# Weight decode through a PSUM bank, a scaling moved to ScalarE, and a new plan of the order, in a fused attention and two-MLP kernel

## The chip, the cores and the metric

One core of one Trainium2 chip runs the whole program. The metric is the device time of one execution in microseconds (us); smaller is better. Engines in the rows: PE is TensorE (PEld its weight loads), DVE VectorE, ACT ScalarE, POOL GpSimd, SP SyncE, which here issues every DMA. An engine name with a q is its instruction queue.

## The reference

Attention with a forget bias, for 4 batches, 8 heads, 576 positions and a head size of 64; then two MLPs over the 2304 tokens of width 512:

```python
cum = np.cumsum(np.maximum(s, 0.0), axis=-1)
scores = scale * q @ k.T + np.minimum(-(cum_q - cum_k), 0.0)     # masked causally
x = softmax(scores) @ v                                          # heads side by side: 2304 x 512
h = x @ w_in                                                     # 512 x 1024
solu = h * softmax(h)
ln = (solu - mean) / sqrt(var + 1e-6) * g_ln
x = ln @ w_out                                                   # 1024 x 512
h = max(x @ w1, x @ w2, x @ w3)                                  # 512 x 768 each
out = h @ w_out2                                                 # 768 x 512
```

The MLP weights arrive as 64-bit floats. The kernel reads each as two 32-bit integers and builds the 32-bit float from them; then it splits it into a high and a low fp16 half, and each product is three fp16 products (high by high, high by low, low by high).

## The kernel before, in words

**Tiles.** The tokens are cut into 18 tiles of 128. A pair of batches has 9: for each of four key blocks j, one tile of either batch, then a tail tile with the last 64 tokens of both. So tiles 0 to 3 use only the first two key blocks. Two tiles make a group; there are 9 groups.

**Steps of a tile.** `prep` (L606) loads q, k and v, splits them into halves (`split_ops`, L370: scaling to the high half L384, L386; low half L413 on DVE or L420 and L423 on POOL) and transposes q and k by DMA (L618, L628). `scores` (L658) makes the products (L684, L690) and the maximum pass (L721, L754). `half` (L764) does the exponential (L773), the split and the transpose by DMA (L792). `values` (L806) multiplies by v (L836, L849), normalizes (L883, L877), splits and transposes (L891). `m1` (L900) is x @ w_in (L915), softmax and LayerNorm (L929 to L977), a split and a transpose by DMA (L984). **Steps of a group:** `m2` (L987: product with w_out L1006, halves L433 and L1023), `m3` (L1027: products with w1, w2, w3 L1045, first result copied L433, running maximum L1064, split), `m4` (L1070: product with w_out2 L1079, output).

**Weights.** `load_w` (L510) handles 40 pieces of 128 x 512 floats (512 KB each): 8 of w_in, 8 of w_out, 18 of w1 to w3 ("w3" in names; piece f, i is columns f of matrix i, in the order f, then i) and 6 of w_out2 ("w2o"). A piece lands in one of four staging buffers, which are halves of the K and V storage (tiles kt and vs in the rows) that belong to key blocks 2 and 3; token tile 4 is the first to store keys there. Three passes on DVE put the bits together: dec1 (L527) into a wide work buffer, a tile of the pool "f" of three; dec2 (L530) in that buffer; dec3 (L533) back into the staging buffer. `split_ops` then scales the staging buffer to the high half (ACT, DVE or POOL) and makes the low half (DVE L413 or POOL L420, L423). w_out is scaled by g_ln, a value per partition, the others by a constant.

**Prologue.** `prologue` (L450) loads s, scales it and cuts it at zero (L474 on DVE), scans it (L476), splits it into three bf16 parts (L483, L486) and writes them to DRAM (L488), from where `load_c` (L491) reads them as operands of the score products. POOL meanwhile fills constants (L459 to L470).

**PSUM.** Eight banks: two for scores (sc), one for values (av), two for h, and three (pool "acc", not first in first out) for m2, m3 and m4. An m3 bank holds one matrix for two columns f: 24 products, 12 for each of two weight pieces.

**The order.** `build` (L331) lists operations with their engines, durations in ns, what they read and write, and a due position `pos` in units of token tiles. `Schedule.run` (L141) plays them on a model: of what could start within `look` ns of the earliest start on an engine it takes the lowest `pos`; where several engines can do an operation, `spare` adds to each engine's end time before it chooses (three numbers up to the position `spare_until`, three after it). Buffers of a pool are given out as they become free. Operations that use the SBUF port which DVE and POOL share in this model are kept apart in time, except the kinds listed in `ALONE` (L96). The resulting order is written out per engine, so each engine runs a fixed list; a waiting instruction holds what stands behind it on its engine, DMA issues on SP too. `P` (L30) holds the positions: wi, wo, w3, w4 the first piece of w_in, w_out, w1 to w3 and w_out2 and wid, wod, w3d, w4d the step from piece to piece; la, lp, lu, lv attention, o1 to o4 and ds the MLP steps, mp the LayerNorm.

Of the kernel before, what the change touches and what calls it, by code (L numbers as in the profile page):

```python
# [29 lines left out]
P = dict(  # L30
    la=4.705,
    lp=-0.544,
    lu=2.19,
    lv=-2.704,
    o1=0.295,
    o2=-2.196,
    o3=1.33,
    o4=0.194,
    ds=2.217,
    wi=-8.083,  # L40
    wid=-0.055,
    wo=0.504,
    wod=1.507,
    w3=-3.448,
    w3d=1.657,
    w4=-4.056,
    w4d=3.311,
    mp=1.816,
    look=[0.0, 0.0, 0.0, 315.4, 20.3],
    spare=[1717.6, 14.8, 1096.8, 262.7, -659.2, -218.5, 5.6],  # L50
    n_st=4,
    avn=1,
    gs=[2, 2, 2, 2, 2, 2, 2, 2, 2],
# [3 lines left out]
    nr=3,  # L57
    lc=-0.912,
    S=[],
# [32 lines left out]
class Schedule:  # L92
    LAT_SAME, LAT_CROSS, LAT_DMA, LAT_ISSUE = 130, 180, 930, 650


    ALONE = frozenset("ttr m1max m3x xn x2l x2h m3c ob rec scan m1v gs".split())  # L96

# [8 lines left out]

    def op(self, alts, reads, writes, pos, dma=0, kind=""):

        o = Op()
        o.unit = self.unit + "." if dma else self.unit  # L110
        o.cls = f"{kind}@{self.tile}"
        only = self.eng.get(o.cls)
        o.alts = [(e, int(ns + 0.5), f) for e, ns, f in alts if not only or e[0] in only]
        o.base, o.dma, o.kind = pos, int(dma + 0.5), kind
        o.pos = pos + self.off.get(o.unit, 0.0)
        o.index = len(self.ops)
        o.deps, o.after, o.bufs = set(), set(), {}
        for k in reads:
            o.deps.update(self.last.get(k, ()))
            self.readers.setdefault(k, []).append(o)  # L120
        for k in writes:
            if k in self.readers or k in self.last:
                o.deps.update(self.readers.get(k, ()))
                o.deps.update(self.last.get(k, ()))
            self.last[k] = [o]
            self.readers[k] = []
        for k in list(reads) + list(writes):
            b = k[0] if isinstance(k, tuple) else k
            if isinstance(b, Buf):
                self.hold(o, b)  # L130
        o.deps.discard(o)
        self.ops.append(o)
        return o
# [7 lines left out]
    def run(self):  # L141
# [6 lines left out]
        dma = 0  # L148
        port = [0]
        busy, warm = {}, [False]  # L150

        def ports(o, e):

            return e == "POOL" or e == "DVE" and o.kind not in self.ALONE

        def clock(t, ns):
# [93 lines left out]
        for _ in self.ops:  # L250
# [10 lines left out]
            t, o, i, e = best  # L261
            ns, o.fn = o.alts[i][1:]
            o.start, o.eng = t, e
            if o.dma:
# [66 lines left out]
def build(nc, T, X, dims):  # L331
# [22 lines left out]
    op = S_.op  # L354
    pools = {}
    for name, n, fifo in (
# [5 lines left out]
        ("mn", 4, True), ("den", 2, True), ("st8", 2, True),  # L362
        ("sc", 2, True), ("av", P["avn"], True), ("h", 1, True), ("acc", 4 - P["avn"], False),
    ):
# [85 lines left out]
    def prologue():  # L450
# [16 lines left out]
        def tri():  # L467
# [5 lines left out]
        op([("POOL", 500, tri)], ["maskt"], ["maskt"], p0, kind="mask")  # L473
        op([("DVE", 369, lambda: nc.vector.tensor_scalar(  # L474
            out=spt(), in0=spt(), scalar1=S_MUL, scalar2=0.0, op0=ALU.mult, op1=ALU.max))], [sp], [sp], p0, kind="relu0")
        op([("DVE", 669, lambda: nc.vector.tensor_tensor_scan(  # L476
# [33 lines left out]
    def load_w(src, hi, lo, scale, pos, wkey, extra=()):  # L510
# [6 lines left out]
        for i in range(nsrc):  # L517
# [7 lines left out]


        op([("DVE", dve1(512), lambda: nc.vector.tensor_scalar(  # L527
            out=t(), in0=high(), scalar1=3, scalar2=0x3FFFFFF8,
            op0=ALU.logical_shift_left, op1=ALU.bitwise_and))], sk, [tb], pos, kind="dec1")
        op([("DVE", dve2(512), lambda: nc.vector.scalar_tensor_tensor(  # L530
            out=t(), in0=low(), scalar=29, in1=t(), op0=ALU.logical_shift_right, op1=ALU.bitwise_or))],
           sk + [tb], [tb], pos, kind="dec2")
        op([("DVE", dve2(512), lambda: nc.vector.scalar_tensor_tensor(  # L533
            out=low(), in0=high(), scalar=-(1 << 30), in1=t(), op0=ALU.bitwise_and, op1=ALU.bitwise_or))],
           sk + [tb], sk, pos, kind="dec3")
        split_ops(lambda g: hi, lambda g: lo, lambda g: low().bitcast(F32), scale, 512,
                  sk + list(extra), [(wkey, 0), (wkey, 1)], pos, k="w", scaled=scaled("w"))

# [119 lines left out]
    def scores(t, h0):  # L658
# [71 lines left out]
        for n, (lo, hi) in enumerate(((0, KH), (KH, S))):  # L730
            sc = [buf("sc") for _ in range(2)]

            def f_sc(n=n, lo=lo, hi=hi, sc=sc):
# [15 lines left out]
               [qt] + ["ktail"] * n + [("kt", i, 2 * n + x) for i in range(2) for x in range(2)] + keyed,  # L749
               sc, pos, kind="sc")  # L750
            for y in range(2):
# [148 lines left out]
    def m1(t):  # L900
# [74 lines left out]
        def ts(eng):  # L975
# [8 lines left out]
        op([("SP", 625, lambda: nc.sync.dma_start_transpose(out=lnt(), in_=lnb()))],  # L984
           [(lnb, 0), (lnb, 1)], [(lb, o)], pos, dma=1792, kind="lnT")

# [141 lines left out]
def fox_attention_solu_max3_kernel(  # L1128
# [59 lines left out]
    for name, n, shape, dt in (  # L1188
# [8 lines left out]
        T[name] = [mk(f"{name}{i}", shape, dt) for i in range(n)]  # L1197
    for name, n, w in (("sc", 2, 512), ("av", P["avn"], 512), ("h", 1, DFF), ("acc", 4 - P["avn"], 512)):
        T[name] = [mk(f"{name}{i}", [128, w], F32, psum) for i in range(n)]
# [39 lines left out]
```

## Time and profile before

| | |
|---|---|
| time before, median of 3 runs | 693.94 us (691.15 to 696.44) |
| the profiled execution's own time | 692.71 us |
| its span in the profile | 690.9 us |
| busy: PE, DVE, ACT, POOL | 598.7, 426.8, 349.4, 107.9 us |
| mean granted TensorE clock | 0.975 of full speed |

The page gives busy time over the whole span, and 40 slices of 17.3 us each, in which a digit is the busy share in tenths. A stage view gives the same for chosen stretches: for each engine the busy us and the number of instructions, then the granted clock, the mean busy share of the 16 DMA engines and what they moved. A group row gives how often an instruction ran, its busy time in all and the mean of one in ns, then the idle time of its engine just before it and what ended that. In a timeline row the first number is the start, the second the duration; instructions on one engine overlap a little, so starts can be closer than durations.

### The profile page before, as it was taken

The numbers are of one execution on the slowest core, as the hardware profiler recorded it, in microseconds if no ns is written. First come the engines' busy times: TensorE is split into PE (matmuls) and PEld (weight loads), VectorE is DVE, ScalarE is ACT, GpSimd is POOL, SyncE is SP. The second block draws the span as 40 slices with busy tenths as digits, with TensorE's granted clock in tenths as the row PEclk, the third lists the DMA queues.
The fourth block names the chain that finished last, engine by engine and source line by source line (L and its number), as shares of the span: only waits on it lengthen the run. The fifth ranks groups of instructions, "written<-read, shape, count | busy, mean of one in ns | idle before, by whom it ended". The sixth has DMA issues, their size and how long they took to land.

```text
span 690.9 us, 15166 instructions
## 1 busy us (share of the span) xinstructions
PE 598.7 (87%) x6028; PEld 425.2 (62%) x6028; DVE 426.8 (62%) x970; ACT 349.4 (51%) x784; POOL 107.9 (16%) x132
## 2 busy tenths in 40 slices
PE   0126658969889999999999999999999999999997
PEld 0012326747456657866676667676867686786784
DVE  6899899998767764747287538733774253143121
ACT  1457665356667763737475638633853244144111
POOL 4003300010103312333133103001121010000000
PEclk9999767989999999999999999999999999999999
DMA  6999998658999994788899947753665040210201
GB/s 174 238 259 242 185 235 203 193 139 191 180 163 171 168 197 91 116 134 145 161 185 177 173 94 129 132 93 62 128 97 96 32 81 16 56 32 8 48 15 31
DMA packets 283016, 91.07 MB, mean 132 GB/s; under 512 B 259136, under 2 KB 277760, under 8 KB 282944
## 3 DMA queue, kind: packets, MB, share of 16 engines
q1 hardware_dynamic: 282944, 90.10, 66.2%
q8 instruction: 47, 0.77, 0.5%
q14 instruction: 25, 0.20, 0.1%
HBM read 35.95 MB, written 4.83 MB: 59 GB/s over the span
## 4 chain that ended last, share of the span: by engine, by line
PE 52%; DMA 23%; DVE 13%; ACT 4%; issue 3%; SPq 3%; POOL 1%; DVEq 0%; ACTq 0%
PE acc L1045 20%; PE acc L1006 9%; DMA et<-es 9%; PE h L915 8%; DMA lnt<-ln 4%; PE acc L1079 4%; PE sc L690 4%; PE av L849 3%; PE sc L684 2%; DVE f L530 2%; DVE es L413 1%; DMA kt<-in_moe_w_dram 1%; PE av L836 1%; DMA ett<-est 1%; DMA raw<-in_q_dram 1%
## 5 line engine op out<-in xcount | busy, mean ns | idle before, releaser
L1045 PE MATMUL acc<-x2A,w_h 128*128 128x256 f16 x1296 | 218.8, 274 | 6.9 <-DVE w_h L413 5.2
L1045 PEld LDWEIGHTS <-w_h 128*128 128x128 f16 x1944 | 187.1, 98 | 39.1 <-DVE w_h L413 6.1
L1045 PE MATMUL acc<-x2B,w_h 128*128 128x256 f16 x648 | 177.5, 274 | 0.0
L915 PE MATMUL h<-w_in_h,xt 128*128 128x512 f16 x432 | 106.4, 393 | 12.0 <-DMA xt<-xs 11.9
L1006 PE MATMUL acc<-lnt,w_out_h 128*128 128x256 f16 x864 | 98.9, 276 | 12.5 <-DMA lnt<-ln 11.7
L773 ACT ACTIVATE r<-r,mn 128x128 f32<-128x128 f32 (+4 forms) x144 | 82.7, 575 | 41.1 <-DVE mn L721 28.7
L1006 PEld LDWEIGHTS <-w_out_h 128*128 128x128 f16 x864 | 84.8, 99 | 26.8 <-issue 12.8
L413 DVE SCALAR_TENSOR_TENSOR es<-r,es 128x512 f16<-128x512 f32 (+1 forms) x92 | 65.9, 723 | 24.7 <-ACT es L384 21.3
L915 PEld LDWEIGHTS <-xt 128*128 128x128 f16 x432 | 40.6, 100 | 60.3 <-DMA xt<-xs 12.9
L384 ACT ACTIVATE es<-r 128x512 f16<-128x512 f32 (+1 forms) x94 | 54.1, 585 | 32.0 <-DMA et<-es 31.3
L721 DVE CUSTOM_DVE_ANT_0 r<-sc,mask 128x128 f32<-128x128 f32 (+3 forms) x128 | 58.1, 485 | 17.4 <-PE sc L690 16.2
L849 PE MATMUL av<-vs,et 128*128 128x64 f16 x960 | 39.5, 197 | 29.9 <-DMA et<-es 28.7
L1079 PE MATMUL acc<-w2o_h,h2A 128*128 128x512 f16 x216 | 64.3, 379 | 0.0
L1064 DVE TENSOR_TENSOR f<-f,acc 128x512 f32<-128x512 f32 x54 | 36.9, 684 | 43.5 <-PE acc L1045 41.7
L849 PEld LDWEIGHTS <-et 128*128 128x128 f16 x960 | 35.7, 100 | 38.4 <-DMA et<-es 32.2
L1023 DVE SCALAR_TENSOR_TENSOR x2B<-acc,x2A 128x512 f16<-128x512 f32 x18 | 12.4, 689 | 64.2 <-ACT x2A L433 64.1
L684 PE MATMUL sc<-ckr,cqr 6*128 6x128 bf16 (+5 forms) x192 | 27.0, 312 | 25.1 <-DMA cqr<-cum_d 24.3
L690 PE MATMUL sc<-kt,qt 64*128 64x256 f16 (+2 forms) x768 | 48.3, 268 | 0.0
L433 ACT ACTIVATE x2A<-acc 128x512 f16<-128x512 f32 x18 | 10.7, 596 | 62.2 <-PE acc L1006 62.2
L1079 PE MATMUL acc<-w2o_h,h2B 128*128 128x512 f16 x108 | 40.9, 379 | 0.0
L384 ACT ACTIVATE h2A<-f 128x512 f16<-128x512 f32 x25 | 15.6, 626 | 47.3 <-DVE f L1064 47.3
L690 PEld LDWEIGHTS <-qt 64*128 64x128 f16 (+1 forms) x864 | 27.2, 100 | 15.9 <-issue 9.1
(111 smaller groups left out, 718.9 us busy)
## 6 DMA issues: line engine op xcount, KB each, us to landing
kt<-in_moe_w_dram SPq DMA_DIRECT2D x18, 256.0 KB
vs<-in_moe_w_dram SPq DMA_DIRECT2D x18, 256.0 KB
raw<-in_k_dram SPq DMA_DIRECT2D x16, 256.0 KB
raw<-in_q_dram SPq DMA_DIRECT2D x16, 256.0 KB
raw<-in_v_dram SPq DMA_DIRECT2D x16, 256.0 KB
out_dram<-f SPq DMA_DIRECT2D x16, 256.0 KB
vs<-in_moe_w_out_dram SPq DMA_DIRECT2D x7, 512.0 KB
kt<-in_moe_w_out_dram SPq DMA_DIRECT2D x7, 512.0 KB
```

Source lines behind the costliest of these rows:

```text
L384: eng.activation(out=out(g), in_=src(g), func=AF.Copy, scale=sc(g))
L413: nc.vector.scalar_tensor_tensor(out=lo(g), in0=src(g), scalar=sc1(g), in1=hi(g), op0=ALU.mult, op1=ALU.subtract)
L684: yield lambda: nc.tensor.matmul(out=out(), lhsT=T["cqr"][cr, hp, cs], rhs=T["ckr"][cr, hp, ck], start=True, stop=False, skip_group_check= ...
L690: yield lambda n=n, qa=qa, o=o, kx=kx: nc.tensor.matmul(out=out()[:, o], lhsT=qv()[r, qa * HP + hp, ts], rhs=kx, start=False, stop=(n == 2 ...
L721: nc.vector.tensor_tensor_reduce(out=gw(R)[:, g], in0=gw(sc[y])[:, g], in1=T["mask"][:, SM - W:SM], scale=1.0 / S_MUL, scalar=3e38, op0=AL ...
L773: nc.scalar.activation(out=gw()[:, g], in_=gw()[:, g], func=AF.Exp, bias=mnf()[:, g:g + 1], scale=-1.0, accum_out=den(hs[g]),)
L849: nc.tensor.matmul(out=out, lhsT=ea_[:, ea, kb], rhs=T["v_s"][c, kb // 2][:, kb % 2, ha + a, va], start=(kb == 0 and m == 0), stop=(kb == ...
L915: nc.tensor.matmul(out=hb()[:, n * 512:(n + 1) * 512], lhsT=xt()[:, xa, kk], rhs=T["w_in_h"][:, wa, kk, n * 512:(n + 1) * 512], start=(kk ...
L1006: nc.tensor.matmul(out=ps()[:, d % 2 * GN:(d % 2 + 1) * GN], lhsT=T["w_out_h"][:, wa, kk, d * 128:(d + 1) * 128], rhs=lnt()[:, la, kk], st ...
L1045: nc.tensor.matmul(out=ps()[:, f % 2 * GN:(f % 2 + 1) * GN], lhsT=T["w123_h"][:, w, wa, f, kk], rhs=x2(xa)[:, kk], start=(kk == 0 and i == ...
L1064: op([("DVE", dve2(2 * GN), lambda ps=ps: nc.vector.tensor_tensor(out=m(), in0=m(), in1=ps(), op=ALU.max))], pk + [m], [m], pos, kind="m3x")
L1079: nc.tensor.matmul(out=ps(), lhsT=h2(ha)[:, f, o * 128:(o + 1) * 128], rhs=T["w2o_h"][:, wa, f], start=(f == 0 and i == 0), stop=(f == KF2 ...
```

## The change

1. In `load_w` dec2 writes an "acc" PSUM bank instead of the work buffer, dec3 works in that bank, and both halves are made from it: the high half on ACT only, the low half on DVE only. The work buffer is read last by dec2, the staging buffer by dec3.
2. The first scaling of s runs on ACT as a Relu with a scale.
3. The planner's model: switching TensorE between score products and other products costs 95, 150 or 300 ns; DMA latency is 1250 instead of 930 ns; the LayerNorm transpose takes 2200 instead of 1792 ns; dec3 and the low half ("wl") no longer count as users of the shared port.
4. All positions in `P` are new, and so is the order of everything.

The pool of "av" was of size P["avn"] = 1 and is now written as 1, "acc" as 3.

```diff
 P = dict(
-    la=4.705, lp=-0.544, lu=2.19, lv=-2.704,
-    o1=0.295, o2=-2.196, o3=1.33, o4=0.194, ds=2.217,
-    wi=-8.083, wid=-0.055, wo=0.504, wod=1.507,
-    w3=-3.448, w3d=1.657, w4=-4.056, w4d=3.311, mp=1.816,
-    look=[0.0, 0.0, 0.0, 315.4, 20.3],
-    spare=[1717.6, 14.8, 1096.8, 262.7, -659.2, -218.5, 5.6],
+    la=10.467, lp=-3.933, lu=3.473, lv=-4.007,
+    o1=-5.042, o2=-6.852, o3=2.269, o4=0.122, ds=5.562,
+    wi=-14.577, wid=-2.374, wo=-5.08, wod=-0.141,
+    w3=0.541, w3d=0.309, w4=-4.008, w4d=5.211, mp=-0.033,
+    look=[0.0, 0.0, 0.0, 213.2, 19.2],
+    spare=[2262.6, -562.2, 1965.8, 458.7, -1447.5, 987.2, 10.4],
...
-    LAT_SAME, LAT_CROSS, LAT_DMA, LAT_ISSUE = 130, 180, 930, 650
+    LAT_SAME, LAT_CROSS, LAT_DMA, LAT_ISSUE = 130, 180, 1250, 650
-    ALONE = frozenset("ttr m1max m3x xn x2l x2h m3c ob rec scan m1v gs".split())
+    ALONE = frozenset("ttr m1max m3x xn x2l x2h m3c ob rec scan m1v gs dec3 wl".split())
...
+        def turn(o, e):
+            if e != "PE" or (o.kind == "sc") == (rows[0][:2] == "sc"):
+                return 0
+            return 95 if o.kind == "sc" else 300 if rows[0] == "sct" else 150
...
             ns, o.fn = o.alts[i][1:]
+            t = max(t, free[e] + turn(o, e))
...
-        op([("DVE", 369, lambda: nc.vector.tensor_scalar(
-            out=spt(), in0=spt(), scalar1=S_MUL, scalar2=0.0, op0=ALU.mult, op1=ALU.max))], [sp], [sp], p0, kind="relu0")
+        op([("ACT", 640, lambda: nc.scalar.activation(out=spt(), in_=spt(), func=AF.Relu, scale=S_MUL))],
+           [sp], [sp], p0, kind="relu0")
...
+        pb = buf("acc")
+        f32 = lambda: pb().rearrange("p (b n) -> p b n", b=8)
+        i32 = lambda: pb().bitcast(I32).rearrange("p (b n) -> p b n", b=8)
...
         op([("DVE", dve2(512), lambda: nc.vector.scalar_tensor_tensor(
-            out=t(), in0=low(), scalar=29, in1=t(), op0=ALU.logical_shift_right, op1=ALU.bitwise_or))],
-           sk + [tb], [tb], pos, kind="dec2")
+            out=i32(), in0=low(), scalar=29, in1=t(), op0=ALU.logical_shift_right, op1=ALU.bitwise_or))],
+           sk + [tb], [pb], pos, kind="dec2")
         op([("DVE", dve2(512), lambda: nc.vector.scalar_tensor_tensor(
-            out=low(), in0=high(), scalar=-(1 << 30), in1=t(), op0=ALU.bitwise_and, op1=ALU.bitwise_or))],
-           sk + [tb], sk, pos, kind="dec3")
-        split_ops(lambda g: hi, lambda g: lo, lambda g: low().bitcast(F32), scale, 512,
-                  sk + list(extra), [(wkey, 0), (wkey, 1)], pos, k="w", scaled=scaled("w"))
+            out=i32(), in0=high(), scalar=-(1 << 30), in1=i32(), op0=ALU.bitwise_and, op1=ALU.bitwise_or))],
+           sk + [pb], [pb], pos, kind="dec3")
+        sc = scale if callable(scale) else (lambda g: scale)
+        px = 107 if callable(scale) else 0
+        op([("ACT", act(512, True) + px, lambda: nc.scalar.activation(out=hi, in_=f32(), func=AF.Copy, scale=sc(0)))],
+           [pb] + list(extra), [(wkey, 0)], pos, kind="wh")
+        op([("DVE", dve2(512) + px * 0.57, lambda: nc.vector.scalar_tensor_tensor(
+            out=lo, in0=f32(), scalar=sc(0), in1=hi, op0=ALU.mult, op1=ALU.subtract))],
+           [pb, (wkey, 0)] + list(extra), [(wkey, 1)], pos, kind="wl")
...
-           [(lnb, 0), (lnb, 1)], [(lb, o)], pos, dma=1792, kind="lnT")
+           [(lnb, 0), (lnb, 1)], [(lb, o)], pos, dma=2200, kind="lnT")
```

## Rows read from the trace of the kernel before

**Rows 1.** The page: TensorE's busy time, and its 40 slices in tenths.
```profile
PE 598.7 (87%) x6028; PEld 425.2 (62%) x6028; DVE 426.8 (62%) x970; ACT 349.4 (51%) x784; POOL 107.9 (16%) x132
...
PE   0126658969889999999999999999999999999997
```
**Rows 2.** Busy time by stage; columns as in the section on the profile.
```profile
0.00:107.00 107.00, 39.35 (x346) 19.53 (x347) 92.73 (x212) 56.29 (x137) 23.33 (x23) 0.89 0.99 221
107.00:157.00 50.00, 43.14 (x339) 33.54 (x337) 46.79 (x89) 25.81 (x46) 1.84 (x2) 0.91 0.67 184
157.00:187.00 30.00, 27.32 (x277) 18.21 (x277) 24.65 (x59) 17.81 (x43) 0.64 (x1) 0.97 0.87 166
187.00:690.90 503.90, 488.88 (x5075) 353.90 (x5071) 262.67 (x614) 249.53 (x560) 82.05 (x106) 1.00 0.59 106
```
**Rows 3.** Timelines of VectorE and TensorE, 45 to 158 us.
```profile
106.81 12.60 PE L1006 MATMUL acc<-lnt,w_out_h 128*128 128x256 f16 x96 [8.57 <-DMA lnt<-ln]
...
106.97 0.74 DVE L413 SCALAR_TENSOR_TENSOR w_out_h<-vs,g_sb,w_out_h 128x512 f16<-128x512 f32 x1
...
156.48 0.69 DVE L413 SCALAR_TENSOR_TENSOR w_h<-vs,w_h 128x512 f16<-128x512 f32 x1
```
**Rows 4.** TensorE's waits, 0 to 190 us: us in total, times, longest.
```profile
PE acc L1006 <- DMA lnt<-ln: 8.6, 1, 8.6
...
PE acc L1006 <- ACT f L433: 0.7, 1, 0.7
```
**Rows 5.** Timeline of the first 14 us, all engines.
```profile
2.69 2.02 POOL L460 MEMSET cqr<- 128x2304 bf16 x1
2.77 2.25 DVE L474 TENSOR_SCALAR ln<-ln 32x576 f32<-32x576 f32 x1 [2.77 <-DMA ln<-in_s_dram]
4.57 0.63 ACT L384 ACTIVATE st<-raw 128x512 f16<-128x512 f32 x1 [2.55 <-DMA raw<-in_k_dram]
...
6.80 0.67 DVE L413 SCALAR_TENSOR_TENSOR st<-raw,st 128x512 f16<-128x512 f32 x1
...
8.90 0.58 SPq L518 DMA_DIRECT2D vs<-in_moe_w_in_dram  x1
...
13.60 0.43 DVE L527 TENSOR_SCALAR f<-vs 128x512 int32<-128x512 int32 x1 [3.14 <-DMA vs<-in_moe_w_in_dram]
```
**Rows 6.** Groups of instructions by line and shape, whole span.
```profile
L1023 DVE SCALAR_TENSOR_TENSOR x2B<-acc,x2A 128x512 f16<-128x512 f32 x18 | 12.4, 689 | 64.2 <-ACT x2A L433 64.1
L433 ACT ACTIVATE x2A<-acc 128x512 f16<-128x512 f32 x18 | 10.7, 596 | 62.2 <-PE acc L1006 62.2
L413 DVE SCALAR_TENSOR_TENSOR w_h<-vs,w_h 128x512 f16<-128x512 f32 x9 | 6.2, 684 | 0.1
L384 ACT ACTIVATE w_h<-kt 128x512 f16<-128x512 f32 x9 | 6.0, 667 | 4.0 <-DVE kt L533 4.0
L423 POOL TENSOR_TENSOR w_h<-kt,w_h 128x512 f16<-128x512 f32 x1 | 1.2, 1163 | 0.1
```
**Rows 7.** Groups of VectorE's instructions, 0 to 157 us.
```profile
L533 DVE SCALAR_TENSOR_TENSOR kt<-kt,f 128x512 int32<-128x512 int32 x19 | 13.4, 705 | 0.0
L533 DVE SCALAR_TENSOR_TENSOR vs<-vs,f 128x512 int32<-128x512 int32 x17 | 13.0, 767 | 0.1
L413 DVE SCALAR_TENSOR_TENSOR es<-r,es 128x512 f16<-128x512 f32 x11 | 9.3, 852 | 0.0
L527 DVE TENSOR_SCALAR f<-kt 128x512 int32<-128x512 int32 x19 | 8.0, 421 | 4.6 <-DMA kt<-in_moe_w_dram 2.1 <-DMA kt<-in_moe_w_in_dram 1.9 <-DMA kt<-in_moe_w_out_dram 0.5
L527 DVE TENSOR_SCALAR f<-vs 128x512 int32<-128x512 int32 x17 | 7.2, 422 | 7.0 <-DMA vs<-in_moe_w_in_dram 3.1 <-POOL ln L423 2.1 <-DMA vs<-in_moe_w_dram 1.6
```
**Rows 8.** Timeline of VectorE: the first piece of weights.
```profile
14.06 0.69 DVE L530 SCALAR_TENSOR_TENSOR f<-vs,f 128x512 int32<-128x512 int32 x1
14.79 0.69 DVE L533 SCALAR_TENSOR_TENSOR vs<-vs,f 128x512 int32<-128x512 int32 x1
...
16.46 0.68 DVE L413 SCALAR_TENSOR_TENSOR w_in_h<-vs,w_in_h 128x512 f16<-128x512 f32 x1
```

More of the change, by code (lines that the diff above doesn't have):

```diff
@@ L30 @@
 P = dict(
[L31 to L48, printed above, removed]
-    look=[0.0, 0.0, 0.0, 315.4, 20.3],
-    spare=[1717.6, 14.8, 1096.8, 262.7, -659.2, -218.5, 5.6],
+    la=10.467,
+    lp=-3.933,
+    lu=3.473,
+    lv=-4.007,
+    o1=-5.042,
+    o2=-6.852,
+    o3=2.269,
+    o4=0.122,
+    ds=5.562,
+    wi=-14.577,
+    wid=-2.374,
+    wo=-5.08,
+    wod=-0.141,
+    w3=0.541,
+    w3d=0.309,
+    w4=-4.008,
+    w4d=5.211,
+    mp=-0.033,
+    look=[0.0, 0.0, 0.0, 213.2, 19.2],
+    spare=[2262.6, -562.2, 1965.8, 458.7, -1447.5, 987.2, 10.4],
     n_st=4,
-    avn=1,
     gs=[2, 2, 2, 2, 2, 2, 2, 2, 2],
@@ L57 @@
     nr=3,
-    lc=-0.912,
+    lc=-1.328,
     S=[],
@@ L105, in __init__, with op @@
         self.unit, self.tile = "", ""
-    def op(self, alts, reads, writes, pos, dma=0, kind=""):
+    def op(self, alts, reads, writes, pos, dma=0, kind="", mode=""):
         o = Op()
@@ L113, in op @@
         o.alts = [(e, int(ns + 0.5), f) for e, ns, f in alts if not only or e[0] in only]
-        o.base, o.dma, o.kind = pos, int(dma + 0.5), kind
+        o.base, o.dma, o.kind, o.mode = pos, int(dma + 0.5), kind, mode
         o.pos = pos + self.off.get(o.unit, 0.0)
@@ L148, in run @@
         dma = 0
-        port = [0]
+        port, rows = [0], [""]
         busy, warm = {}, [False]
@@ L272, in run @@
                 free[e] = o.end = clock(t, ns) if e == "PE" else t + ns
+                if e == "PE":
+                    rows[0] = o.kind + o.mode
                 if ports(o, e):
@@ L362, in build @@
         ("mn", 4, True), ("den", 2, True), ("st8", 2, True),
-        ("sc", 2, True), ("av", P["avn"], True), ("h", 1, True), ("acc", 4 - P["avn"], False),
+        ("sc", 2, True), ("av", 1, True), ("h", 1, True), ("acc", 3, False),
     ):
@@ L749, in scores @@
                [qt] + ["ktail"] * n + [("kt", i, 2 * n + x) for i in range(2) for x in range(2)] + keyed,
-               sc, pos, kind="sc")
+               sc, pos, kind="sc", mode="t")
             for y in range(2):
@@ L1197, in fox_attention_solu_max3_kernel @@
         T[name] = [mk(f"{name}{i}", shape, dt) for i in range(n)]
-    for name, n, w in (("sc", 2, 512), ("av", P["avn"], 512), ("h", 1, DFF), ("acc", 4 - P["avn"], 512)):
+    for name, n, w in (("sc", 2, 512), ("av", 1, 512), ("h", 1, DFF), ("acc", 3, 512)):
         T[name] = [mk(f"{name}{i}", [128, w], F32, psum) for i in range(n)]
```

## The prediction

> **What bounds the kernel now.** I read the page's busy shares and slices first, then busy time by stage, then what TensorE waited for, and last the decode's own rows and the first 14 us.
>
> TensorE is busy 598.7 of 690.9 us, and the slices show where it is not: the first ten, some 170 us, are thin, the rest full [rows 1]. The stages say it exactly [rows 2]. Up to 107 us TensorE works 39.4 us and stands 67.6; from 107 to 157 it stands 6.9, from 157 to the end 533.9 - 27.3 - 488.9 = 17.7. So the end is the moment from which TensorE is fed, plus work that hardly has a gap. The reader is to see in the same rows who is full while TensorE starves: VectorE works 92.7 + 46.8 = 139.5 of the first 157 us, and the DMA engines' share is 0.99 up to 107.
>
> What TensorE starts on at 106.81 is the first w_out product, which waited for the transposed LayerNorm output of tile 1; on VectorE the last low half of w_out begins only at 106.97 [rows 3]. That wait is 8.6 us; a wait of this product for a free accumulator bank is 0.7 us in all [rows 4]. After it the 18 w1/w2/w3 tiles come one by one from the decode; the last low half of one begins at 156.48 [rows 3], which is why I cut at 157. Keys of token tile 4 go into the staging buffers, so nothing later can begin before the 40 decodes are through. Up to 157 us what VectorE saves moves the whole rest forward nearly one for one; after that only TensorE's own gaps can be won.
>
> **The change part by part.** The sum is made against the profiled execution, 692.7 us (span 690.9 and 1.8 around it); it lies 0.2% under the median of 693.9, so no correction is needed.
>
> *First scaling on ScalarE.* On VectorE it took 2.25 us, from 2.77, while GpSimd's second large memset ran from 2.69 [rows 5]. On ScalarE, which has no scaling to do until 4.57, I take 0.7 us: a 128x512 scaling there takes 0.67 [rows 6], this one has 576 columns on fewer partitions. The scan starts about 1.4 us sooner; VectorE's low half of the keys (6.80) comes sooner too, and with it, on SP, the first weight load at 8.90. VectorE's first decode at 13.60 waits 3.14 us for that load, so the start moves with it. Gain 1.4; between 0 (the DMAs are late anyway) and 1.5.
>
> *Third and fourth pass read the bank.* dec3 and the low half have one SBUF operand less and no longer meet GpSimd there. dec3 means are 705 and 767 ns against the usual 684 [rows 6, 7]: 19 x 0.021 + 17 x 0.083 = 1.8 us up to 157, which go. dec2 still has two SBUF operands and keeps its share. At most the planner also puts GpSimd work beneath these passes and frees the es rows, 11 x (0.852 - 0.684) = 1.8 more. At worst 0. I take 1.8.
>
> *Price of the bank for VectorE.* No row shows VectorE writing PSUM. Reading it, the same operation on 128x512 takes 689 ns [rows 6] against 684 from SBUF: 5 ns. For dec2, dec3 and the low half of the 36 tiles before 157: 108 x 5 ns = 0.5 us. Bounds: 0, and 108 x (767 - 684) = 9.0 if every pass became as slow as the worst dec3 group; I stay by the nearest row.
>
> [...]
>
> *High half on ScalarE from the bank.* 596 against 667 ns [rows 6], 36 x 0.07 = 2.5 us less on ScalarE. It works 56.3 + 25.8 of 157 us [rows 2], so it is not the bound: nothing. If it queued behind other ScalarE work it would hold the bank, see below.
>
> *Low half off GpSimd.* One of the low halves was GpSimd's (1163 ns); now it is 0.68 on VectorE, before 157: +0.6. Bounds 0 and 0.7.
>
> *Staging buffers free after dec3.* In the first decode dec3 ends at 15.48 and the low half at 17.14 [rows 8]: the buffer is free 1.7 us sooner, and SP's load of the next weights, with all that is queued behind it on SP, goes sooner. VectorE stood for weights before dec1 4.6 us (kt) and 2.1 + 1.6 + 3.1 us (vs); 3.1 is the first load and 2.1 GpSimd's [rows 7]. So at most 4.6 + 1.6 = 6.2 are refills, in several waits, mostly under 1.7 us each. Since the DMA engines are full up to 107 us, part of it would come back as a longer transfer. I take 4; bounds 0 and 6.2. The third wide buffer ("f") is freed after dec2 as well, which I count at nothing.
>
> *A bank as a new wait.* dec2 must have an accumulator bank, and keeps it until the low half is done; m2, m3 and m4 have the same three. Until 107 us no product uses them, so it is free. Then an m3 accumulator opens when the first of its two weight tiles is ready and closes with the second. What is queued behind a waiting dec2 is all of VectorE (score maxima, LayerNorm passes), and TensorE waits for those. Today's wait for a bank is 0.7 us; I take +1. Below: 0. Above: the decode of all 18 m3 weights one after the other through one bank, 3.08 us from dec2 to the end of the low half [rows 8], 0.07 less for ScalarE, some 0.1 to hand over, 3.1 against VectorE's own 0.42 + 3 x 0.684 = 2.47: 18 x 0.64 = 11.5.
>
> *The order.* It is the largest unknown. The new due times put w_out (from -5.1 in steps of -0.14, was 0.5 in steps of 1.5) and tile 1's LayerNorm ahead of the w1/w2/w3 tiles, which then come close together (steps of 0.31, was 1.66). Today both wait behind early w1 to w3 decodes, and the 8.6 us wait is what comes of it. But the same VectorE work must be done by 157: an earlier start of the w_out product meets weights that are not there. So the 8.6 us are not a gain by themselves. What can be gained is 17.7 + 6.9 us of TensorE's gaps after 107, where longer DMA latencies and TensorE's turns now enter the plan. I take a sixth, 4 us. Bounds: 12 (half of them), and a loss of 10, about the size of that 8.6 us wait once more: the planner's times are not the chip's.
>
> Sum: -1.4 - 1.8 + 0.5 + 0.6 - 4 + 1 - 4 = -9.1; 692.7 - 9.1 = **683.6 us**.
>
> **The rivals.**
> *A: the order and the loads give nothing.* The DMA share of 0.99 and the conservation of VectorE's work speak for it, the many short stands of VectorE and TensorE against it. Without the two terms of 4, and with the bank at 1: 692.7 - 1.4 - 1.8 + 1.1 + 1 = 691.6 us, not to be told from before.
>
> *B: the accumulator banks become the bound.* Place: VectorE's dec2 and TensorE's m3 from about 100 us to the last w1/w2/w3 tile. m3 opens two of three banks with half its weights and decodes pass one at a time through the third. For it: three banks for four users, and m3's weights come in the order f, then w, so all accumulators of a pair open before one closes. Against it: VectorE has other work for the gaps, and the planner counts the banks. Price 11.5 instead of 1, loads and order gaining nothing: 692.7 - 1.4 - 1.8 + 1.1 + 11.5 = 702.1 us. It decides from about 8 us of lost VectorE time, 0.45 us a tile, which eats up the other terms.
>
> *C: the order does much more.* GpSimd beneath dec3 and low half (1.8 more), all refills (2.2 more) and half of TensorE's gaps (8 more) go: 683.6 - 12 = 671.6 us. For it: 17.5 us of VectorE idle before 157; against: TensorE is 97% busy from 157 on.
>
> **How the numbers follow.** Forecast 0.48, C 0.14, A 0.26, B 0.12. A measurement of this kernel tells about 1% from no change: below 687.0 or above 700.9 us. The forecast and C are faster, A is the same, B slower: 0.62, 0.26, 0.12. The range leaves out the outermost part of B and of C, to 670 below and 697 above, which holds about 8 in 10; the forecast's own range is 677 to 689.
>
> **What would show it.** Right: the first L474 operation on ScalarE below 1 us and the scan before 4 us; dec3 and low half between 0.68 and 0.70 us with no stretched ones; VectorE's stands for weight loads under 3 us in all; the last w1/w2/w3 low half before 150 us; TensorE's gaps after it under 15 us. Wrong: dec2 standing behind a release of a bank by 0.4 us or more a tile (B); the last w1/w2/w3 low half still at 157 us with the DMA share at 1 (A); dec3 or low half above 0.72 us (the price of PSUM); TensorE's busy time grown by a lower granted clock, which is 0.89 up to 107 us today and would fall if an earlier product stood for weights.

## The result and the profile after

The changed kernel takes 687.93 us, median of 6 runs (686.43 to 688.42), against 693.83 us (691.15 to 696.44) for the kernel before on the same chip: a ratio of 0.991, 95% interval 0.9884 to 0.9935. The profiled execution takes 686.43 us (span 684.7); the one before took 692.71 (span 690.9). So 5.9 us were gained by the medians and 6.3 by the profiled executions, of 9.1 forecast. The direction was right and the time lies in the range, at the upper edge of the forecast's own one (677 to 689). It lies above the 687.0 under which the prediction would have called this kernel faster, and a little nearer to rival A (691.6) than to the forecast (683.6). But the interval excludes 1, so a gain of some 6 us is shown, at two thirds of the forecast size.

The page after, TensorE's busy time and slices; they answer to [rows 1]:

```profile
PE 598.2 (87%) x6028; PEld 425.6 (62%) x6028; DVE 421.6 (62%) x994; ACT 358.4 (52%) x810; POOL 58.1 (8%) x63
...
PE   0126666989999999899999999998999999999997
```

Busy time by stage after. The first four rows have the cuts of [rows 2]; the next two are cut where the last w1/w2/w3 low half ends.

```profile
0.00:107.00 107.00, 42.68 (x344) 20.06 (x344) 90.24 (x216) 58.08 (x141) 23.67 (x28) 0.89 1.05 235
107.00:157.00 50.00, 42.19 (x347) 33.74 (x348) 48.00 (x94) 24.98 (x47) 0.45 (x1) 0.93 0.79 195
157.00:187.00 30.00, 29.39 (x329) 22.09 (x328) 21.77 (x52) 19.69 (x48) 3.41 (x4) 1.00 1.00 167
187.00:684.70 497.70, 483.98 (x5015) 349.68 (x5013) 261.62 (x635) 255.66 (x577) 30.61 (x31) 1.00 0.57 103
...
0.00:150.70 150.70, 78.86 (x632) 49.07 (x633) 131.97 (x298) 80.43 (x183) 23.67 (x28) 0.90 0.99 226
150.70:684.70 534.00, 519.38 (x5398) 376.50 (x5395) 289.65 (x698) 277.98 (x627) 34.46 (x35) 1.00 0.59 107
```

The same cut in the kernel before:

```profile
0.00:157.20 157.20, 82.69 (x683) 53.07 (x683) 139.72 (x300) 82.10 (x182) 25.17 (x25) 0.90 0.89 210
157.20:690.90 533.70, 516.00 (x5346) 372.11 (x5345) 287.12 (x671) 267.34 (x602) 82.68 (x107) 1.00 0.60 109
```

The decode ends 6.5 us earlier, and what comes after it is as long as before (534.0 against 533.7), though 3.4 us more of TensorE's work is left for it. TensorE stands 150.70 - 78.86 = 71.8 us ahead of the cut (before 74.5) and 14.6 behind it (before 17.7): 2.7 and 3.1 us less, and 0.5 us less work make the 6.2 us of the span, up to rounding. At the fixed cuts of [rows 2] the larger part lies early: up to 107 us TensorE stands 64.3 us instead of 67.6, after that 22.1 instead of 24.6. VectorE does 7.7 us less ahead of the cut. But the column to look at is the last but one: the DMA engines' share is 0.99 over the whole decode, where it was 0.89. GpSimd's work has halved (58.1 us, before 107.9), nearly all of that behind the cut.

VectorE, ScalarE and TensorE after, a timeline; the second, third and fifth row answer to [rows 5, 8] and [rows 3]:

```profile
2.64 0.68 ACT L482 ACTIVATE ln<-ln 32x576 f32<-32x576 f32 x1 [0.63 <-DMA ln<-in_s_dram]
...
3.36 1.35 DVE L484 TENSOR_TENSOR_SCAN e<-ln 32x576 f32<-32x576 f32 x1 [3.36 <-ACT ln L482]
...
13.21 0.43 DVE L539 TENSOR_SCALAR f<-vs 128x512 int32<-128x512 int32 x1 [4.04 <-DMA vs<-in_moe_w_in_dram]
...
111.51 7.05 PE L1023 MATMUL acc<-lnt,w_out_h 128*128 128x256 f16 x48 [6.78 <-DMA lnt<-ln]
...
150.03 0.68 DVE L552 SCALAR_TENSOR_TENSOR w_h<-acc,w_h 128x512 f16<-128x512 f32 x1
```

The scaling is short and early, as said, and the scan starts at 3.36, where the scaling alone ended at 5.02 before (2.77 + 2.25); but the first decode starts at 13.21 instead of 13.60, because it waits 4.04 us for its load instead of 3.14. The first w_out product starts at 111.51, later than the 106.81 of before.

The decode's groups after, whole span; they answer to [rows 6, 7]:

```profile
L542 DVE SCALAR_TENSOR_TENSOR acc<-vs,f 128x512 int32<-128x512 int32 x20 | 14.6, 728 | 0.1
...
L542 DVE SCALAR_TENSOR_TENSOR acc<-kt,f 128x512 int32<-128x512 int32 x20 | 13.9, 695 | 0.1
...
L545 DVE SCALAR_TENSOR_TENSOR acc<-vs,acc 128x512 int32<-128x512 int32 x20 | 13.8, 689 | 0.1
...
L545 DVE SCALAR_TENSOR_TENSOR acc<-kt,acc 128x512 int32<-128x512 int32 x20 | 13.8, 689 | 0.1
...
L552 DVE SCALAR_TENSOR_TENSOR w_h<-acc,w_h 128x512 f16<-128x512 f32 x18 | 12.1, 683 | 0.0
...
L550 ACT ACTIVATE w_h<-acc 128x512 f16<-128x512 f32 x18 | 10.5, 589 | 10.0 <-DVE acc L545 9.9
```

dec3 (705 and 767 ns before) no longer stretches, and a bank that is read and written costs it 689 ns. The low half reads the bank and writes SBUF in 683 ns, where it took 684 from SBUF.

VectorE's waits ahead of dec1, 0 to 190 us (us in total, times, longest). VectorE has no wait for a bank in this trace:

```profile
DVE f L539 <- DMA vs<-in_moe_w_in_dram: 4.9, 2, 4.0
DVE f L539 <- DMA kt<-in_moe_w_dram: 2.1, 2, 1.5
DVE f L539 <- DMA kt<-in_moe_w_out_dram: 0.6, 1, 0.6
```

### The profile page after: what moved, and what is told of

Its sections match the earlier page's. It is cut to its first block, busy times and chain, and to the rows that moved or that the text cites. A ratio compares the mean times of both kernels' runs of the same rounds, so it can differ in the third digit from the quotient of the medians.

```text
span 684.7 us, 15120 instructions
## 1 busy us (share of the span) xinstructions
PE 598.2 (87%) x6028; PEld 425.6 (62%) x6028; DVE 421.6 (62%) x994; ACT 358.4 (52%) x810; POOL 58.1 (8%) x63
## 4 chain that ended last, share of the span: by engine, by line
PE 61%; DMA 14%; DVE 9%; issue 9%; ACT 4%; SPq 1%; POOL 1%; POOLq 0%; DVEq 0%; ACTq 0%
PE acc L1062 23%; PE acc L1023 11%; PE h L932 10%; PE acc L1096 8%; DMA et<-es 4%; PE sc L707 4%; DMA vs<-in_moe_w_in_dram 2%; DMA xt<-xs 2%; PE av L866 2%; DMA qt<-st 2%; PE sc L701 2%; DMA lnt<-ln 2%; DVE acc L542 1%; PE av L853 1%; ACT r L790 1%
## 5 line engine op out<-in xcount | busy, mean ns | idle before, releaser
L1062 PE MATMUL acc<-x2A,w_h 128*128 128x256 f16 x1296 | 216.4, 273 | 3.3 <-DVE f L1081 3.0
L1023 PE MATMUL acc<-lnt,w_out_h 128*128 128x256 f16 x864 | 99.4, 275 | 6.8 <-DMA lnt<-ln 6.8
L392 ACT ACTIVATE es<-r 128x512 f16<-128x512 f32 (+1 forms) x104 | 59.9, 588 | 24.9 <-DMA et<-es 24.2
L1096 PE MATMUL acc<-w2o_h,h2A 128*128 128x512 f16 x216 | 64.3, 379 | 0.0
L866 PE MATMUL av<-vs,et 128*128 128x64 f16 x960 | 39.8, 197 | 18.0 <-DMA et<-es 17.7
L441 ACT ACTIVATE f<-acc 128x512 f32<-128x512 f32 x45 | 26.6, 591 | 34.0 <-PE acc L1062 22.4
L701 PEld LDWEIGHTS <-cqr 6*128 6x128 bf16 (+1 forms) x192 | 8.2, 95 | 49.4 <-POOL vs L431 23.7
```

What stands on the lines that cost most here:

```text
L392: eng.activation(out=out(g), in_=src(g), func=AF.Copy, scale=sc(g))
L701: yield lambda: nc.tensor.matmul(out=out(), lhsT=T["cqr"][cr, hp, cs], rhs=T["ckr"][cr, hp, ck], start=True, stop=False, skip_group_check= ...
L866: nc.tensor.matmul(out=out, lhsT=ea_[:, ea, kb], rhs=T["v_s"][c, kb // 2][:, kb % 2, ha + a, va], start=(kb == 0 and m == 0), stop=(kb == ...
L1023: nc.tensor.matmul(out=ps()[:, d % 2 * GN:(d % 2 + 1) * GN], lhsT=T["w_out_h"][:, wa, kk, d * 128:(d + 1) * 128], rhs=lnt()[:, la, kk], st ...
L1062: nc.tensor.matmul(out=ps()[:, f % 2 * GN:(f % 2 + 1) * GN], lhsT=T["w123_h"][:, w, wa, f, kk], rhs=x2(xa)[:, kk], start=(kk == 0 and i == ...
L1096: nc.tensor.matmul(out=ps(), lhsT=h2(ha)[:, f, o * 128:(o + 1) * 128], rhs=T["w2o_h"][:, wa, f], start=(f == 0 and i == 0), stop=(f == KF2 ...
```

## The experiments

In the table "end" is the end of the last w1/w2/w3 low half, "VectorE" its busy time up to there, "rest" the span after it, "m2" the start of the first w_out product, all in us. The medians come from several chips, so kernels are compared by their ratio to the kernel before, run beside them; the other columns are of the one profiled execution.

| kernel | median | ratio (95%) | end | VectorE | rest | m2 |
|---|---|---|---|---|---|---|
| before | 693.83 | | 157.2 | 139.7 | 533.7 | 106.8 |
| after | 687.93 | 0.9910 (0.9884 to 0.9935) | 150.7 | 132.0 | 534.0 | 111.5 |
| e1, scratch in SBUF | 687.02 | 0.9894 (0.9857 to 0.9931) | 149.9 | 136.6 | 535.6 | 110.2 |
| e2, scaling on VectorE | 687.60 | 0.9903 (0.9869 to 0.9937) | 151.4 | 133.5 | 533.9 | 111.9 |
| e3, new decode, old plan | 691.83 | 0.9951 (0.9930 to 0.9972) | 148.8 | 128.0 | 542.0 | 118.7 |
| e4, old decode, new plan | 698.35 | 1.0063 (1.0040 to 1.0086) | 150.7 | 128.8 | 548.7 | 111.1 |
| e5, after, light passes | 687.59 | 0.9902 (0.9871 to 0.9934) | 149.6 | 99.4 | 533.1 | 111.1 |
| e6, after, light loads | 678.63 | 0.9775 (0.9742 to 0.9808) | 141.3 | 132.3 | 534.2 | 101.4 |
| e7, buffers held in the plan | 695.92 | 1.0024 (1.0001 to 1.0046) | 152.3 | 135.7 | 541.0 | 114.1 |
| e8, buffers held in fact | 702.25 | 1.0108 (1.0067 to 1.0150) | 155.2 | 137.7 | 545.7 | 114.3 |
| e9, before, light dec2 | 691.28 | 0.9956 (0.9934 to 0.9979) | 154.1 | 125.1 | 534.5 | 105.8 |
| e10, before, light loads | 681.05 | 0.9787 (0.9764 to 0.9810) | 148.2 | 138.4 | 531.3 | 99.4 |
| e11, no turn times | 682.06 | 0.9802 (0.9767 to 0.9836) | 152.5 | 132.2 | 528.1 | 112.4 |
| e12, positions drawn anew | 687.14 | 0.9883 (0.9857 to 0.9909) | 151.7 | 133.3 | 533.2 | 111.0 |

**The bank as such (e1).** The order of after; the half-decoded weights lie in three SBUF tiles that are still unused then.

```diff
+    pt = lambda: T["scratch"][pb.slot]      # k_tail and two parts of v_tail
-    f32 = lambda: pb().rearrange("p (b n) -> p b n", b=8)
+    f32 = lambda: pt().bitcast(F32).rearrange("p (b n) -> p b n", b=8)
     ...  # i32 likewise
```

> The order of the changed kernel, instruction for instruction, but the half-decoded weights lie in spare SBUF (2 KB a piece of the tail's K and V storage, unused until the decode is over) instead of a PSUM bank. Theory 1 (VectorE's work ahead of the last w1 to w3 piece shrank because its passes no longer meet GpSimd): passes of over 1 us come back among dec2, dec3 and the low halves, the last w1 to w3 low half is 2 to 4 us later than 150.0, the time 690 to 692 us. Theory 2 (the new order makes the gain, the place of the bits is neutral): 687 to 689 us, the last low half within 1 us.

VectorE's groups of dec3 and of one low half in this kernel:

```profile
L546 DVE SCALAR_TENSOR_TENSOR v_tail<-kt,v_tail 128x512 int32<-128x512 int32 x15 | 11.1, 740 | 0.1
...
L553 DVE SCALAR_TENSOR_TENSOR w_h<-v_tail,w_h 128x512 f16<-128x512 f32 x12 | 8.9, 742 | 0.0
...
L546 DVE SCALAR_TENSOR_TENSOR k_tail<-kt,k_tail 128x512 int32<-128x512 int32 x5 | 4.8, 955 | 0.0
```

The stretched passes are back, up to 955 ns in the mean, and VectorE works 4.6 us more up to the cut. The time does not move: 0.9894 against 0.9910, a difference of 1.1 us the other way with an error of some 3 from the two intervals, and the decode ends no later (149.9). The bank does what the prediction said it does, and that is worth nothing measurable.

**The scaling (e2).** The order of after; the instruction runs on VectorE.

```diff
-    op([("ACT", 640, lambda: nc.scalar.activation(out=spt(), in_=spt(), func=AF.Relu, scale=S_MUL))],
+    op([("ACT", 640, lambda: nc.vector.tensor_scalar(
+        out=spt(), in0=spt(), scalar1=S_MUL, scalar2=0.0, op0=ALU.mult, op1=ALU.max))],
```

> The order of the changed kernel, with the first scaling of s emitted on VectorE again. The prediction's term: +1.4 us, 689.3. Reading of the trace after: VectorE's first decode waits for its load in any case (4.0 us), so only some 0.4 us come back: 688.0 to 688.6 us, first decode near 13.6 us.

It takes 2.22 us again; the first decode starts at 14.33, 1.1 us later than after, and the decode ends 0.7 us later. The time is the same (0.9903, error some 3 us), so moving it is worth nothing that can be told.

**Decode and plan crossed (e3, e4).** e3 keeps the new decode and scaling, planned with the old positions, latencies and no turn times. e4 keeps everything new but the decode.

```diff
 # e3, in short
-    P = dict(la=10.467, ...)  LAT_DMA 1250, turn 95/150/300, lnT 2200
+    P = dict(la=4.705, ...)   LAT_DMA 930, turn 0, lnT 1792
 # e4, dec2 shown; dec3, both halves and ALONE also as before
-            out=i32(), in0=low(), scalar=29, in1=t(), op0=ALU.logical_shift_right, op1=ALU.bitwise_or))],
-           sk + [tb], [pb], pos, kind="dec2")
+            out=t(), in0=low(), scalar=29, in1=t(), op0=ALU.logical_shift_right, op1=ALU.bitwise_or))],
+           sk + [tb], [tb], pos, kind="dec2")
```

> Decode through the bank, dec3 and low half free of the port rule, scaling on ScalarE, but the positions, latencies and turn costs of the kernel before (planned anew with them). Theory 1 (the decode makes the gain): 686 to 690 us, last w1 to w3 low half before 152. Theory 2 (the positions and the turn times make it): 692 to 696 us.

> Decode in SBUF as before (dec3 into the staging buffer, halves on any engine), with the new positions, latencies and turn costs, scaling on ScalarE. Theory 1: no gain, 692 to 698 us. Theory 2: 686 to 690 us.

On 693.8 us the ratios make 690.4 (e3), 698.2 (e4) and 687.6 (after). So the decode is worth 3.4 us in the old plan and 10.6 in the new, and the plan costs 4.4 us with the old decode and gives 2.8 with the new. Each of these has an error of some 2 us from the intervals. The parts do not add up: the new positions need the new decode. The time of e3 falls between the two expectations, that of e4 just beyond both. Busy time by stage, cut at the end of the decode, e3:

```profile
0.00:148.80 148.80, 73.69 (x572) 43.09 (x572) 128.04 (x284) 76.71 (x176) 35.32 (x39) 0.91 0.98 224
148.80:690.80 542.00, 525.74 (x5459) 382.05 (x5456) 285.71 (x682) 272.23 (x613) 75.46 (x99) 1.00 0.58 106
```

and e4:

```profile
0.00:150.70 150.70, 80.83 (x632) 50.61 (x633) 128.76 (x292) 79.56 (x180) 15.76 (x18) 0.88 0.95 215
150.70:699.40 548.70, 526.72 (x5396) 378.76 (x5395) 301.21 (x723) 281.43 (x630) 13.16 (x11) 0.99 0.61 107
```

Either part alone ends the decode as early as both do (148.8 and 150.7, before 157.2) and fills the DMA engines (0.98 and 0.95). e4 gets there although its low half still reads the staging buffer, so an early end does not need the early release. What only both together keep is the rest: 534.0 us. In e3 6.4 us more of TensorE's work is left for it; in e4 TensorE stands 22.0 us behind the cut instead of 14.6 and works 7.3 us longer.

Part of e4's loss is a lower clock in the middle of the run; its mean clock is 0.960 to 0.968 in all nine executions, 0.978 to 0.982 after. Two stretches, and two runs of products of one shape, in e4:

```profile
400.00:410.00 10.00, 6.30 (x64) 4.08 (x62) 9.16 (x23) 9.19 (x22) 0.00 (x0) 0.84 1.01 180
410.00:420.00 10.00, 10.00 (x83) 5.50 (x82) 4.83 (x13) 3.80 (x11) 0.00 (x0) 0.81 0.67 135
...
408.47 6.63 PE L924 MATMUL h<-w_in_h,xt 128*128 128x512 f16 x18 [2.04 <-DMA xt<-xs]
...
416.64 1.47 PE L924 MATMUL h<-w_in_h,xt 128*128 128x512 f16 x6
```

TensorE stands 3.7 of 10 us, and the granted clock falls to 0.84 and 0.81; from 420 to 450 us it is 1.00. After the stand 18 products take 6.63 us, 368 ns each; six of the same shape take 1.47 us, 245 ns each, 8 us later. TensorE's busy time in e4 is 607.5 us against 598.2. Each cell of this square is a single order, so these are the worths of these four kernels, not of decode and plan in general.

**Is VectorE the pace? (e5, e9)** e5 is after, with dec1 to dec3 of 36 of the 40 pieces (all but the first four, of w_in) on an eighth of their columns; the scale of these pieces, save w_out's, is zero. e9 is before, with dec2 alone of the same 36 on an eighth.

```diff
 # e5, dec1 to dec3
+    cut = 8 if n_w[0] <= 4 else 1
-    out=t(), in0=high(), scalar1=3, scalar2=0x3FFFFFF8,
+    out=cb(t()), in0=cb(high()), scalar1=3, scalar2=0x3FFFFFF8,      # cb = lambda a: a[:, 0:cut]
     ...  # dec2, dec3 likewise
-    sc = scale if callable(scale) else (lambda g: scale)
+    sc = scale if callable(scale) else (lambda g, z=(scale if cut == 8 else 0.0): z)
 # e9, dec2
-    out=t(), in0=low(), scalar=29, in1=t(), ...
+    out=t()[:, 0:cut], in0=low()[:, 0:cut], scalar=29, in1=t()[:, 0:cut], ...
```

> The order of the changed kernel; from the fifth piece of weights on dec1, dec2 and dec3 work on 64 of 512 columns (the weights come out wrong; w1 to w3 and w_out2 become zeros). 36 x 3 passes lose most of their time, some 36 x 1.4 = 50 us of VectorE. Theory 1 (VectorE sets the pace up to the last w1 to w3 piece, as the prediction says): that piece 15 us or more earlier than 150.7, the time 670 us or less. Theory 3 (transfers set it, since with SBUF scratch 4.6 us more of VectorE's work moved nothing): under 4 us earlier, the time 683 to 688 us.

> The kernel before in its own order; from the fifth piece of weights on dec2 works on 64 of 512 columns, so the lowest three bits of most weights are left out. 36 x 0.6 = some 21 us less on VectorE, about 19 of them before the last w1 to w3 piece (157.2). Theory 1 (VectorE sets the pace there, the base of the prediction): that piece 10 us or more earlier, the time 684 us or less. Theory 3 (the loads set it in this order too): at most 3 us earlier, 691 to 695 us.

Busy time by stage up to the cut, e5:

```profile
0.00:149.60 149.60, 75.66 (x627) 48.21 (x628) 99.43 (x298) 79.69 (x183) 23.31 (x28) 0.92 0.98 227
```

and e9:

```profile
0.00:154.10 154.10, 83.24 (x683) 53.58 (x683) 125.10 (x300) 81.97 (x182) 26.23 (x25) 0.89 0.91 213
```

In e5 VectorE has 32.5 us less to do, stands a third of the stage, and the decode ends 1.1 us sooner; the time is that of after. In e9 14.6 us less make the decode end 3.1 us sooner. So a us saved on VectorE is worth 0.03 us in e5 and 0.2 in e9. VectorE is not the pace, in the new kernel least of all; the DMA share stays at 0.98 and 0.91.

**Are the loads the pace? (e6, e10)** The same two orders; the loads of the same 36 pieces bring an eighth of the bytes (w1 to w3 a quarter), and the passes run whole, on what lies in the buffers.

```diff
+    cut = 8 // nsrc if n_w[0] <= 4 else 1
-    out=st().rearrange("p (k x) n -> p k x n", x=nsrc)[:, :, i], in_=src[i]))],
+    out=st().rearrange("p (k x) n -> p k x n", x=nsrc)[:, :, i][:, 0:cut], in_=src[i][:, 0:cut]))],
```

> The order of the changed kernel; from the fifth piece of weights on a load brings a part of its data (1/8 of w_in, w_out and w_out2, 1/4 of w1 to w3), the rest of the staging buffer is what was there. VectorE's work is whole. Theory 1: the last w1 to w3 piece at most 5 us earlier, the time 683 to 688 us. Theory 3: that piece and the first w_out product (111.5) 8 us or more earlier, the time 679 us or less.

> The kernel before in its own order; from the fifth piece on a load brings a part of its data (1/8 of w_in, w_out and w_out2, 1/4 of w1 to w3). Theory 1: at most 5 us faster, the size of VectorE's waits for weights. Theory 3: 8 us or more faster, 686 us or less, the first w_out product before 100 us.

Busy time by stage, e6:

```profile
0.00:141.30 141.30, 78.88 (x632) 49.21 (x633) 132.30 (x298) 80.23 (x183) 23.42 (x28) 0.93 0.66 136
141.30:675.50 534.20, 519.14 (x5397) 376.21 (x5395) 288.18 (x697) 277.33 (x627) 34.95 (x35) 1.00 0.59 106
```

and e10:

```profile
0.00:148.20 148.20, 83.40 (x683) 53.16 (x683) 138.40 (x300) 81.86 (x182) 25.38 (x25) 0.90 0.60 128
```

With VectorE's work unchanged the decode ends 9.4 us sooner in the new order and 9.0 in the old. Only now is VectorE nearly full (9.0 and 9.8 us idle). By the ratios the light loads give (0.9910 - 0.9775) x 693.8 = 9.4 us after, and 14.8 us before. The difference, 5.4 us, has an error of some 3, from the three intervals, and it would mean that most of the gain is made on the loads: with light loads the two kernels are alike by the ratios (0.9775 and 0.9787). The traces do not bear that out. With light loads the new kernel still ends its decode 6.9 us sooner than the old one (141.3 and 148.2) and its span is 4.0 us shorter (675.5 and 679.5; with full loads 6.5 and 6.2). So the pair shows that the loads set the end of the decode in both orders, not how much of the gain they carry.

**Early release of the buffers (e7, e8).** e7 has the new decode, but its plan keeps a staging buffer until the low half is done. e8 has e7's order and also does it: dec3 writes back into the staging buffer and the halves are made from there.

```diff
 # e7, wh and wl also read the staging buffer in the plan
-    [pb] + list(extra), [(wkey, 0)], pos, kind="wh")
+    [pb] + sk + list(extra), [(wkey, 0)], pos, kind="wh")
 # e8 = e7 and
-    out=i32(), in0=high(), scalar=-(1 << 30), in1=i32(), ...
+    out=low(), in0=high(), scalar=-(1 << 30), in1=i32(), ...
-    out=hi, in_=f32(), func=AF.Copy, scale=sc(0)
+    out=hi, in_=low().bitcast(F32), func=AF.Copy, scale=sc(0)
```

> Planned as if a staging buffer were held until the low half is done; on the chip it is free after dec3, as the instructions wait only for what they read. It shows what the earlier release is worth to the plan: theory of the prediction 4 us, 692 us; if the planner cannot do without it, 695 us or more; if it is worth nothing, 688.

> The order of the run before this one, but dec3 writes into the staging buffer and both halves are read from there, so that the next load truly waits for the low half. Compared with that run: up to 4 us slower if the earlier release lets loads start sooner on the chip; within 1 us if the loads find the DMA engines full anyway.

What SP's weight loads wait for, 0 to 170 us (us in total, times, longest), e7:

```profile
SPq L526 <- DVE acc L545: 13.4, 7, 4.8
```

and e8:

```profile
SPq L526 <- DVE w_h L552: 19.3, 7, 5.0
...
SPq L526 <- DVE w_out_h L552: 6.8, 3, 2.8
```

The same two by stage, e7 and then e8:

```profile
0.00:152.30 152.30, 78.82 (x656) 50.65 (x657) 135.66 (x297) 80.18 (x184) 24.34 (x28) 0.91 0.97 221
152.30:693.30 541.00, 520.55 (x5373) 375.91 (x5371) 293.30 (x704) 278.84 (x629) 21.49 (x25) 0.99 0.59 106
...
0.00:155.20 155.20, 80.12 (x669) 51.95 (x669) 137.72 (x298) 82.94 (x184) 26.37 (x28) 0.92 0.96 215
155.20:700.90 545.70, 522.56 (x5360) 376.15 (x5359) 293.37 (x704) 279.48 (x629) 21.42 (x25) 0.99 0.59 106
```

Same order, same chip, 6.3 us apart (702.25 - 695.92, error some 3). In e8 the loads wait for the low half, in e7 for dec3, one pass earlier, and the decode ends 152.3 instead of 155.2. That is 2.9 of the 7.6 us between the two spans; the other 4.7 lie behind the cut, where TensorE stands 2.7 us longer and works 2.0 us longer. Whether these too come from the late loads is not shown. e8 also puts two passes back on SBUF; e1 says that this costs nothing by itself, but it said so in another order. And e7 itself is slower than after by 0.0114 x 693.8 = 7.9 us, the second of its expected cases (695 or more). A plan made for late buffers lost the gain even where they come free early, though plans of the same work lie about 1% apart here.

**The turn times, and other positions (e11, e12).** e11 takes the switching costs out of the planner. e12 has other positions, whose planned length is 0.4% under that of after.

```diff
 # e11
-    return 95 if o.kind == "sc" else 300 if rows[0] == "sct" else 150
+    return 0
```

> The changed kernel planned anew without TensorE's turn times, all else as it is. If the turn times carry the gain of the new order: 692 us or more. If they only follow what TensorE does in any case: within 2 us of 687.9.

> The changed kernel with positions drawn anew (the planner's own length is 0.4% shorter). If the plan's length carries over: 685.5 us. If its errors are as large as what it gains: anywhere from 682 to 694 us.

e11 is faster than both kernels, by 2.0% and 1.1%; neither expectation held. The stretches in e11:

```profile
152.50:680.60 528.10, 517.16 (x5398) 375.92 (x5395) 292.02 (x706) 275.98 (x626) 23.37 (x24) 1.00 0.61 108
...
200.00:500.00 300.00, 294.49 (x3445) 203.29 (x3446) 212.99 (x549) 204.88 (x484) 21.59 (x22) 1.00 0.87 148
```

The decode ends 1.8 us later than after, so it's not there: behind the cut TensorE stands 10.9 us instead of 14.6 and works 2.2 us less; from 200 to 500 us it stands 5.5 us, where after stands 9.0. e12 is like after. So one edit of the planner's model shifts the time by a per cent, in a direction that the model doesn't tell. Whether the turn times are wrong as a model, or this order just fell out well, the runs don't settle.

## Why the prediction was right, and where it was not

**The step that failed is the one on which four of the sum's seven terms rest:** "Up to 157 us what VectorE saves moves the whole rest forward nearly one for one". VectorE's 139.5 of 157 us were read as the pace, and the 0.99 of the DMA share beside it as a side condition. It is the other way round: 32.5 us of VectorE's work are worth 1.1 us in the new order (e5), 14.6 are worth 3.1 in the old one (e9), and the transfers are worth 9 in both (e6, e10). VectorE looked full because it is the next limit behind the loads: with light loads it is busy 132.3 of the 141.3 us up to the cut (e6).

- *First scaling, -1.4:* no gain that can be told. The instruction got short as said (0.68 us, scan at 3.36); the first load's arrival decides the rest, the lower bound that the prediction named (e2).
- *Collisions, -1.8:* they went, as the rows of the groups show, and are worth nothing that can be told (e1).
- *Price of the bank, +0.5, and the low half off GpSimd, +0.6:* sizes right (689 and 683 ns), effect nothing that can be told, since VectorE has room. High half on ScalarE: 589 ns, off the path, as said.
- *Staging buffers, -4:* the mechanism is there, its size in this order is not shown. In the order of e7 and e8 the early release is worth 2.9 us at the end of the decode and 6.3 in time. The prediction's upper bound (6.2) was taken from VectorE's stands without the first load; these are 7.6 - 4.0 = 3.6 after, 2.6 us less. The row to read beside them was SP's wait of the loads themselves, 0 to 170 us. In the kernel before it was

```profile
SPq L518 <- DVE w_h L413: 15.7, 10, 2.7
...
SPq L518 <- POOL w_h L423: 2.7, 1, 2.7
...
SPq L518 <- DVE w_out_h L413: 2.3, 3, 1.2
```

  and after it is

```profile
SPq L526 <- DVE acc L545: 14.8, 12, 2.6
```

  Loads that waited 20.7 us for a low half wait 14.8 for dec3 (and 1.0 for low halves). The DMA engines are 0.99 busy through the decode instead of 0.89; the plan without the early release reached 0.95 (e4), so the rise is not the release's alone.
- *Bank wait, +1:* none seen. Rival B (702.1) falls: three banks were enough for four users in this order.
- *Order, -4:* -2.8 with the new decode, +4.4 with the old (e3, e4), each with an error of some 2. The size is near; the place only in part. TensorE's gaps behind the cut went from 17.7 to 14.6, but of the 5.8 us that TensorE stands less 3.3 lie ahead of 107 us, where the prediction looked for nothing from the order. The order gains only on top of the decode, and e11 shows that more lay in a detail of the same plan, 4.1 us by the two spans (684.7 - 680.6) and 0.0108 x 693.8 = 7.5 by the ratios.

That the time came this near is in part luck. The four VectorE terms and the bank wait, -3.2 and +2.1, were not there and nearly cancel, so the forecast rested on the two terms of 4, and of their 8 us about 6 came. How these divide between the early release and the order stays open: e3 and e4 show that neither alone brings the gain, and the release was not taken out of the order of after itself. Rival A was wrong in its time (691.6) and right in its reason, the DMA share of 0.99 up to 107 us; over the whole decode the share was 0.89 and still had room. Rival C (671.6) did not happen.

Of what would show it: scaling, scan and unstretched passes came out as written (only w_out's low halves take 746 ns, as they took 745 before); the stands for weight loads did not (7.6 us, forecast under 3); the last low half starts at 150.03, just beyond the 150 forecast; the gaps after it are 14.6, under 15. The clock up to 107 us is 0.89 as before.

## What to carry to other kernels

That an engine is some 90% busy does not make it the bound. Here VectorE was, 139.7 of 157.2 us, and lighter loads moved the end of the stage by 9.0 us (e10), lighter dec2 passes by 3.1 (e9). So freeze the order, lighten one resource at a time, and see which one moves the end of the stage, before any instruction saved is counted as time. Where loads set the pace, look at when their buffers come free and at what the issue of the load waits for; one pass less between arrival and release was worth 2.9 us at the end of the stage in the one order where it was tried. And where an order is planned anew with each edit, an edit is priced only within a fixed order, since plans of the same work lay about 1% apart here.

## What the runs showed of the hardware

A transpose by DMA took longer among the full loads than among light ones. In the chain of waits of after, the LayerNorm output of tile 1 takes

```profile
104.19 7.28 DMA lnt<-ln
```

and in that of e6, where the loads are light,

```profile
97.00 4.33 DMA lnt<-ln
```

One transpose of q, the same in both orders, holds SP 4.71 us after and 1.38 in e6:

```profile
49.23 4.71 SPq L645 DMA_TRANSPOSE qt<-st  x1
...
48.14 1.38 SPq L646 DMA_TRANSPOSE qt<-st  x1
```

The first w_out product waits for the LayerNorm's transpose (6.78 us after, 5.34 in e6), so the loads delay TensorE not only by weights. Up to the cut VectorE writes PSUM at the price of SBUF within 11 ns (684 against 689 to 695); over the whole span only dec2, which still has two SBUF operands, has a group with a higher mean (728). And stretches of a VectorE pass of up to 955 ns in the mean can be real and cost nothing that can be measured, as e1 shows. They meet GpSimd, as far as its rough spans tell: in the kernel before the three dec3 passes of over 1 us (1.10, 1.66 and 1.09, at 30.73, 59.65 and 82.81 us) have GpSimd busy beside them for 0.6, 1.6 and 1.0 us, though one of 0.69 at 59.04 has it beside it too, for 0.6. After, with dec3 in the bank, five passes have it beside them for 0.6 us, and each takes 0.69 us or less.
